# An RWKV scan with a SoLU layer behind it on one core: from word 502 of the written order on, engine orders and queues are chosen anew, five squares are halved by GpSimd, and four state sums move from TensorE to VectorE

## The chip, the cores and the metric

The kernel runs on one core of a Trainium2 chip. The core has TensorE (PE in the profile, matrix products; its weight loads are shown as PEld), VectorE (DVE), ScalarE (ACT), GpSimd (POOL), and SyncE (SP), which here only issues transfers. The metric is the device time of one execution in microseconds (us); lower is better.

## The reference

The input is four batches of eight heads, 768 steps, head size 48. A linear recurrence runs over the steps; its result, rows of 8 x 48 = 384 values, goes through a layer 384 -> 1024 -> 384 with a SoLU (a softmax times its own input), a layer norm and a gain. In float32:

```python
for t in range(S):                                   # S = 768, for 4 batches and 8 heads
    cur = einsum('bhd,bhe->bhde', u * k[t], v[t])
    y[t] = einsum('bhd,bhde->bhe', r[t], state + cur)
    state = w[t][..., None] * state + einsum('bhd,bhe->bhde', k[t], v[t])
x = y as 3072 rows of 384
h = x @ w_in
sm = softmax(h); solu = h * sm
ln = (solu - mean(solu)) / sqrt(var(solu) + 1e-6) * g_ln
out = ln @ w_out
```

## The kernel before

The 768 steps are cut into 6 chunks of 128, so there are 24 units of work (chunk, batch); unit i is chunk i // 4 of batch i % 4, and unit i needs the state that unit i - 4 left. Everything that the kernel does is one step of one unit, and the order of the steps is written out by hand: the string `ORDER` (line 21) is a list of words such as `Oa17.7`, which means step `Oa` of unit 17 with the option `7`. The loop at line 698 reads the words one after another and calls the step's function. The class `InOrder` (line 70) chains the instructions of each engine, so that each engine executes its instructions exactly in the order of the words; nothing is reordered by a scheduler. Between engines only data and buffers order the work. A buffer is one of a ring (4 to 10 deep, line 67), so a step also waits until the unit that had the buffer before is through with it. PSUM has eight banks, and the digit in an option of a TensorE step is the bank that it writes.

The steps of a unit, with the engine of each, in the order in which one unit goes through them:

- `LW LK LR LV`: the loads, 192 KB each, issued by SP, or by GpSimd (`.g`) or ScalarE (`.a`). `lw`, `ex` (ScalarE): logarithm and exponential of the decays. `cum` (TensorE): two products that sum the logarithms. `kp` (VectorE): k and r times the decays. `kt` (SP): both turned by a transposing transfer (in the first units TensorE does it instead).
- `p`, `q` (GpSimd), `dg` (VectorE), `dv` (GpSimd): the bonus term of u. `vb`: v as bf16, by ScalarE (`.a`) or GpSimd (`.p`).
- `M` (TensorE) and `m` (VectorE): the scores within the chunk and their mask. `Y` (TensorE) and `y`: the chunk's result. With the option `i` the bonus is added by a TensorE product and `y` is copied by ScalarE; else `y` is a VectorE addition.
- `S` (TensorE), `et` (ScalarE), `st` (VectorE): the new state. `S` makes the decay of the chunk and the sum over its steps, and adds the old state with a product with the identity (lines 458 to 480). With the option `n` that product is left out, and `st` (lines 482 to 489) adds the old state on VectorE and then multiplies by the decay; without `n`, `st` is the multiplication alone.
- the turning of y: `X` (three TensorE products) and `xT` (a copy), or `xt` (a transposing transfer by SP).
- `H` (TensorE), `e` (ScalarE, exponential), `he` (VectorE, h times e), `hq` (ScalarE, square): the hidden layer, with the 1024 values along partitions, so 24 products of 128 columns. A unit that has an `ht` word (`by_rows`, line 501) is computed the other way round, with six products of 512 columns, row sums taken by ScalarE, and `he` turned back by a transposing transfer.
- `Oa`, `Ob` (TensorE, lines 610 to 640): the output, in two halves of four blocks. Each block has a product of 386 columns for the output, a narrow one (2 columns) for the sum of e, and a narrow one (1 column) for the sum of the squares. For a unit with a word `ea`, GpSimd adds the two halves of e beforehand and half of the narrow products of e fall away. For a unit with a word `qa` the same holds for the squares:

```python
def square_add(i, x):
    pool.tensor_add(out=hq[:, :KF // 2, :], in0=hq[:, :KF // 2, :], in1=hq[:, KF // 2:, :])
...
if i not in paired:                       # paired: the units with a word qa
    pe.matmul(o_ps[:, DM + 2:], lhsT=hq[:, f, :], rhs=one_col[:, :1], ...)
elif f % 2 == 0:
    pe.matmul(o_ps[:, DM + 2:], lhsT=hq[:, f // 2, :], rhs=one_col[:, :1], ...)
```

- `qm`, `lv`, `rs`, `o`, `out`: variance, its root, the scaled output and the store by SP. Unit 23, the last, is cut in halves (`HA HB EA EB DA DB QA QB`), and its store is shared by ScalarE and SP.

The order before has no `qa` word and no state with `n`. All instructions are recorded by the one helper at line 86, so the profile shows L86 for nearly all of them, and the tiles tell them apart.

Of the kernel before, what the change touches and what calls it, by code (L numbers as in the profile page):

```python
# [41 lines left out]
out5 lw19 dg10 e6 p13 kt15 H7.3 dv11 LV13 LW21.g xT8.a q12 he6 e7 vb12.p H8.6 hq6.a lw16 st11 he7 kt13 dg12  # L42
M12.1 X9.0 Oa6.5 p15 xT9.a dv10 Y11.n3 lw18 LK20.g m12.d Ob6 e8 p14 y11.d qm6 LV17 hq7.a he8 lv6 Y10.n2 LK18
M15.0 m15.d q13 rs6 y10.d dv12 q14 q15 H9.3 Oa7.7 Ob7 o6.a X10.0 LV14.a e9 LV16.g out6 hq8.a xT10.a he9 Y12.n5
p17 lw21 vb15.p vb14.p hq9.a xt11 qm7 y12.d M14.1 S10.3 Oa8.0 cum16.4 m14.d LK21.g et10 lv7 S12.1 st10 rs7
LK19.g LW22 dg15 dg13 Ob8 LR19.g vb13.a xt12 cum18.2 o7.a et12 ex16 H11.6 qm8 lv8 st12 kp16 out7 ex18 rs8 dv15
o8.a e11 dv13 S15.1 et15 dg14 H12.4 ea11.p e12 kp18 vb17.a q17 LR21 vb16.a out8 LV19.g LV21 lw22 he11 kt16
LV18.g hq11.a S13.3 p16 st15 Oa9.0 LR22.g Y15.n7 he12 LR20 y15.d Ob9 LK22 q16 M13.4 cum21.1 qm9 lv9 m13.d ex21
kp21 H10.6 p19 xt15 et13 rs9 Oa11.5 o9.a cum19.0 e10 Ob11 p18 st13 he10 qm11 hq12.a ex19 dg17 out9 Y13.n2 Oa12.4
Ob12 lv11 lw20 y13.d kt18 hq10.a rs11 dv14 vb19.p q18 M16.2 kt17 X13.7 kp19 Y14.n6 qm12 p21 vb18.a LK23 S16.0  # L50
xT13.a S14.7 lv12 rs12 o12.a m16.d y14.d cum20.1 et16 out12 et14 dg16 st14 q19 H13.3 H15.6 dg18 st16 ex20 xt14
o11.a Oa10.5 kp20 e13 dv16 M17.0 out11 ea13.p he13 dg19 cum22.2 e15 p20 ex22 dv17 Y16.i4 he15 Ob10 kp22 y16.a
H14.6 hq13.a e14 qm10 LW23.g q20 p22 M18.3 dv18 q22 ea15.p S18.2 LV20 lv10 kt19 m17.d Y17.n1 m18.d hq15.a Oa13.0
y17.d et18 dg20 st18 Ob13 rs10 he14 M19.3 ea14.p o10.a xt16 vb20.p qm13 H16.1 e16 kt22 dv20 Y18.n6 X17.5 m19.d
lv13 kt20 y18.d out10 xT17.a q21 rs13 Oa15.7 LV22.g Ob15 he16 M20.4 qm15 hq14.a S17.3 lv15 m20.d H17.1 dg21 et17
st17 kt21 M21.5 dv19 rs15 LR23 o15.a e17 m21.d Oa14.4 Ob14 he17 lw23 o13.a qm14 cum23.5 Y19.n3 xt18 Y20.n7 ex23
y19.d lv14 out15 y20.d ht16 LV23 ea17.p vb22.p rs14 vb21.a o14.a H18.0 p23 e18 X20.2 dg22 M22.3 S19.7 hq17.a
kp23 xT20.d m22.d Oa16.6 sv16 dv21 Y21.n5 hq16.a sv18 vb23.a Ob16 sq16 et19 H20.2 out13 he18 q23 y21.d dg23 dv22
e20 st19 xt19 he20 H19.0 Y22.n5 Oa17.7 kt23 e19 dv23 qm16 Ob17 y22.d ht18 M23.4 xt21 he19 lv16 rs16 o16.d Oa18.3
Ob18 hq20.a H21.0 hq18.a hq19.a m23.d ht20 xt22 out14 sq18 sv20 qm18 e21 lv18 ea19.p Y23.n2 rs18 Oa19.6 qm17  # L60
ea21.p lv17 rs17 y23.d Ob19 he21 Oa20.5 hq21.a qm19 out16 H22.0 o17.d xt23 lv19 o18.d rs19 Oa21.2 HA23.3 Ob21
out18 HB23.4 e22 Ob20 o19.d EA23 he22 hq22.a EB23 qm21 sq20 DA23 ea22.p lv21 qm20 lv20 DB23 QB23.d rs21 Oa22.7
QA23.a rs20 out17 Ob22 qm22 o20.a out19 lv22 Oa23.6 o21.d rs22 Ob23.s34 out20 out21 o22.a qm23 lv23 rs23 out22
o23.a out23.h
"""

NIO, NLW, NKP, NWK, NHT = 7, 10, 6, 4, 4
# [664 lines left out]
```

## Time and profile before

| what | value |
|---|---|
| median of 3 runs | 143.83 us (143.63 to 145.34) |
| the profiled execution, its own time | 144.28 us |
| span of the program in the profile | 142.5 us |
| busy: PE, DVE, ACT, POOL | 126.0, 122.7, 118.6, 118.4 us |
| TensorE clock granted, mean | 0.992 |

The span runs from the first instruction of the program to the last; the execution's own time has 1.8 us more around it. A row of the timeline gives the start of an instruction, its length, engine, operation, and output <- inputs. Matmuls overlap: a row of 0.33 us can be followed by the next 0.16 us later. What a group of matmuls costs TensorE is therefore read from the start of the group to the start of the next one. The same holds, less strongly, for the other engines.

### The profile page before, as it was taken

The numbers are of one execution on the slowest core, as the hardware profiler recorded it, in microseconds if no ns is written. First come the engines' busy times: TensorE is split into PE (matmuls) and PEld (weight loads), VectorE is DVE, ScalarE is ACT, GpSimd is POOL, SyncE is SP. The second block draws the span as 40 slices with busy tenths as digits, with TensorE's granted clock in tenths as the row PEclk, the third lists the DMA queues.
The fourth block names the chain that finished last, engine by engine and source line by source line (L and its number), as shares of the span: only waits on it lengthen the run. The fifth ranks groups of instructions, "written<-read, shape, count | busy, mean of one in ns | idle before, by whom it ended". The sixth has DMA issues, their size and how long they took to land.

```text
span 142.5 us, 4827 instructions
## 1 busy us (share of the span) xinstructions
PE 126.0 (88%) x1901; PEld 95.7 (67%) x1906; DVE 122.7 (86%) x203; ACT 118.6 (83%) x243; POOL 118.4 (83%) x152
## 2 busy tenths in 40 slices
PE   0598966968999999999969999999999999999970
PEld 0146545657967887669858797788866766787760
DVE  6147889996999999999987999899999999878760
ACT  3658799959999999999986989998677889897780
POOL 7999999979999999999999999999999693402300
PEclk9999999999999999999999999999999999999996
DMA  4999999999999999999999899999999897562314
GB/s 93 272 300 346 316 282 384 389 293 225 249 249 244 290 250 294 246 224 230 234 191 278 197 230 212 281 158 223 176 218 208 134 246 80 136 182 68 127 59 167
DMA packets 94713, 31.98 MB, mean 224 GB/s; under 512 B 88585, under 2 KB 92818, under 8 KB 94690
## 3 DMA queue, kind: packets, MB, share of 16 engines
q1 hardware_dynamic: 70578, 20.79, 67.9%
q10 hardware_dynamic: 22128, 4.79, 15.6%
q0 software_dynamic: 1984, 6.10, 14.1%
q8 instruction: 15, 0.25, 0.7%
q14 instruction: 8, 0.07, 0.1%
HBM read 22.03 MB, written 4.72 MB: 188 GB/s over the span
## 4 chain that ended last, share of the span: by engine, by line
PE 48%; DMA 16%; POOL 14%; ACT 10%; DVE 5%; issue 3%; ACTq 0%; POOLq 0%; DVEq 0%
PE ps L86 48%; DMA win_f<-in_moe_w_in_dram 5%; DMA kr<-kp 5%; DMA kr_in<-in_r_dram 4%; POOL w L86 3%; DMA xT<-y 3%; POOL q L86 2%; ACT ps L86 2%; ACT hq L86 2%; POOL win_sb L86 1%; POOL p L86 1%; ACT e L86 1%; DVE kr L86 1%; POOL dv L86 1%; DVE he L86 1%
## 5 line engine op out<-in xcount | busy, mean ns | idle before, releaser
L86 PE MATMUL ps<-w,he 128*128 128x386 bf16 (+4 forms) x208 | 43.5, 312 | 0.0
L86 PE MATMUL ps<-xT,win_sb 128*128 128x128 bf16 x504 | 31.2, 219 | 0.2 <-DVE kr L86 0.2
L86 ACT ACTIVATE e<-ps 128x1024 bf16<-128x1024 f32 (+1 forms) x25 | 24.6, 987 | 7.5 <-PE ps L86 6.6
L86 PEld LDWEIGHTS <-win_sb 128*128 128x128 bf16 x504 | 29.0, 98 | 1.8 <-DVE kr L86 0.3
L86 DVE TENSOR_TENSOR kp<-ps,kr_in 128x768 bf16<-128x768 f32 x24 | 22.6, 950 | 7.9 <-DMA kr_in<-in_r_dram 4.2
L86 DVE TENSOR_TENSOR he<-ps,e 128x1024 bf16<-128x1024 f32 (+1 forms) x22 | 25.6, 1170 | 2.2 <-ACT e L86 1.9
L86 DVE TENSOR_TENSOR m<-ps,keep 128x1024 bf16<-128x1024 f32 x22 | 26.6, 1215 | 0.8 <-PE ps L86 0.7
L86 PE MATMUL ps<-one_col,hq 128*128 128x1 bf16 x168 | 26.7, 164 | 0.0
L86 POOL TENSOR_TENSOR p<-kr_in 128x384 bf16<-128x384 f32 x24 | 23.9, 1003 | 0.3
L86 ACT ACTIVATE hq<-he 128x1024 bf16<-128x1024 bf16 (+1 forms) x21 | 21.6, 1031 | 0.7 <-DVE he L86 0.7
L86 POOL TENSOR_TENSOR dv<-vb,dg 128x384 bf16<-128x384 bf16 x24 | 19.8, 829 | 2.6 <-DVE dg L86 2.3
L86 POOL TENSOR_TENSOR q<-p,u_bc 128x384 bf16<-128x384 bf16 x24 | 21.7, 914 | 0.1
L86 PEld LDWEIGHTS <-he 128*128 128x128 bf16 x208 | 19.1, 96 | 3.5
L86 ACT ACTIVATE ps<-ps 128x768 f32<-128x768 f32 x24 | 19.0, 796 | 2.4 <-PE ps L86 2.2
L86 PEld LDWEIGHTS <-hq 128*128 128x128 bf16 x168 | 14.1, 96 | 8.3
L86 POOL TENSOR_TENSOR ea<-e 128x512 bf16<-128x512 bf16 x9 | 10.3, 1150 | 9.4 <-ACT e L86 9.4
L86 ACT ACTIVATE lw<-w_in 128x384 bf16<-128x384 f32 x24 | 12.3, 521 | 5.5 <-DMA w_in<-in_w_dram 5.5
L86 PE MATMUL ps<-inv_col,e 128*128 128x2 bf16 x96 | 15.1, 165 | 0.0
L86 PEld LDWEIGHTS <-kp 128*128 128x128 bf16 x176 | 12.2, 104 | 3.9 <-DVE kp L86 2.1
L86 PEld LDWEIGHTS <-kr 64*128 64x128 bf16 (+1 forms) x272 | 10.3, 96 | 6.1 <-issue 1.8
L86 DVE TENSOR_REDUCE dg<-q 128x8 f32<-128x384 bf16 x24 | 12.8, 542 | 0.0
L86 POOL DMA_DIRECT2D kr_in<-in_r_dram x12 | 11.0, 921 | 0.3 <-POOL p L86 0.3
(97 smaller groups left out, 271.5 us busy)
## 6 DMA issues: line engine op xcount, KB each, us to landing
out_dram<-o SPq DMA_DIRECT2D x23, 192.0 KB, 3.2
kr_in<-in_k_dram SPq DMA_DIRECT2D x13, 192.0 KB, 5.1
kr_in<-in_r_dram POOLq DMA_DIRECT2D x12, 192.0 KB, 5.1
w_in<-in_w_dram SPq DMA_DIRECT2D x11, 192.0 KB, 5.2
kr_in<-in_r_dram SPq DMA_DIRECT2D x10, 192.0 KB, 5.3
v_in<-in_v_dram SPq DMA_DIRECT2D x10, 192.0 KB, 5.5
v_in<-in_v_dram POOLq DMA_DIRECT2D x9, 192.0 KB, 4.2
w_in<-in_w_dram ACTq DMA_DIRECT2D x8, 192.0 KB, 3.6
```

The costliest lines, as they stand in the source:

```text
L86: made = make(*args, **kwargs)
```

## The change

Only `ORDER` changes. Its first 501 words (up to `Y12.n5`) stay, and with them every engine's program up to there, which in the profile is the time up to about 78 us. Behind them all words are placed anew:

- `qa` for units 14, 16, 17, 19 and 21 (GpSimd halves their squares).
- `S12`, `S13`, `S17` and `S19` get `n`: the old state is added by VectorE.
- Unit 16 loses `ht`, `sv` and `sq`: it goes the usual way instead of by rows. It gets `ea`; so does unit 12, while 11 and 14 lose theirs.
- Units 11 and 12 are turned by TensorE (`X`, `xT`) instead of a transfer, unit 17 by a transfer instead of TensorE.
- Twelve instead of eight loads go to GpSimd's queue behind the split (`.g`). `vb14`, `vb15` and `vb20` go from GpSimd to ScalarE, `vb17` and `vb23` the other way; `y16` goes from ScalarE to VectorE, `y18` the other way; `xT20` and `o16` go from VectorE to ScalarE.
- The engines' orders, the queues' orders and the banks behind the split are new.

```diff
@@ -42,26 +42,26 @@
 out5 lw19 dg10 e6 p13 kt15 H7.3 dv11 LV13 LW21.g xT8.a q12 he6 e7 vb12.p H8.6 hq6.a lw16 st11 he7 kt13 dg12
 M12.1 X9.0 Oa6.5 p15 xT9.a dv10 Y11.n3 lw18 LK20.g m12.d Ob6 e8 p14 y11.d qm6 LV17 hq7.a he8 lv6 Y10.n2 LK18
 M15.0 m15.d q13 rs6 y10.d dv12 q14 q15 H9.3 Oa7.7 Ob7 o6.a X10.0 LV14.a e9 LV16.g out6 hq8.a xT10.a he9 Y12.n5
-p17 lw21 vb15.p vb14.p hq9.a xt11 qm7 y12.d M14.1 S10.3 Oa8.0 cum16.4 m14.d LK21.g et10 lv7 S12.1 st10 rs7
-LK19.g LW22 dg15 dg13 Ob8 LR19.g vb13.a xt12 cum18.2 o7.a et12 ex16 H11.6 qm8 lv8 st12 kp16 out7 ex18 rs8 dv15
-o8.a e11 dv13 S15.1 et15 dg14 H12.4 ea11.p e12 kp18 vb17.a q17 LR21 vb16.a out8 LV19.g LV21 lw22 he11 kt16
-LV18.g hq11.a S13.3 p16 st15 Oa9.0 LR22.g Y15.n7 he12 LR20 y15.d Ob9 LK22 q16 M13.4 cum21.1 qm9 lv9 m13.d ex21
-kp21 H10.6 p19 xt15 et13 rs9 Oa11.5 o9.a cum19.0 e10 Ob11 p18 st13 he10 qm11 hq12.a ex19 dg17 out9 Y13.n2 Oa12.4
-Ob12 lv11 lw20 y13.d kt18 hq10.a rs11 dv14 vb19.p q18 M16.2 kt17 X13.7 kp19 Y14.n6 qm12 p21 vb18.a LK23 S16.0
-xT13.a S14.7 lv12 rs12 o12.a m16.d y14.d cum20.1 et16 out12 et14 dg16 st14 q19 H13.3 H15.6 dg18 st16 ex20 xt14
-o11.a Oa10.5 kp20 e13 dv16 M17.0 out11 ea13.p he13 dg19 cum22.2 e15 p20 ex22 dv17 Y16.i4 he15 Ob10 kp22 y16.a
-H14.6 hq13.a e14 qm10 LW23.g q20 p22 M18.3 dv18 q22 ea15.p S18.2 LV20 lv10 kt19 m17.d Y17.n1 m18.d hq15.a Oa13.0
-y17.d et18 dg20 st18 Ob13 rs10 he14 M19.3 ea14.p o10.a xt16 vb20.p qm13 H16.1 e16 kt22 dv20 Y18.n6 X17.5 m19.d
-lv13 kt20 y18.d out10 xT17.a q21 rs13 Oa15.7 LV22.g Ob15 he16 M20.4 qm15 hq14.a S17.3 lv15 m20.d H17.1 dg21 et17
-st17 kt21 M21.5 dv19 rs15 LR23 o15.a e17 m21.d Oa14.4 Ob14 he17 lw23 o13.a qm14 cum23.5 Y19.n3 xt18 Y20.n7 ex23
-y19.d lv14 out15 y20.d ht16 LV23 ea17.p vb22.p rs14 vb21.a o14.a H18.0 p23 e18 X20.2 dg22 M22.3 S19.7 hq17.a
-kp23 xT20.d m22.d Oa16.6 sv16 dv21 Y21.n5 hq16.a sv18 vb23.a Ob16 sq16 et19 H20.2 out13 he18 q23 y21.d dg23 dv22
-e20 st19 xt19 he20 H19.0 Y22.n5 Oa17.7 kt23 e19 dv23 qm16 Ob17 y22.d ht18 M23.4 xt21 he19 lv16 rs16 o16.d Oa18.3
-Ob18 hq20.a H21.0 hq18.a hq19.a m23.d ht20 xt22 out14 sq18 sv20 qm18 e21 lv18 ea19.p Y23.n2 rs18 Oa19.6 qm17
-ea21.p lv17 rs17 y23.d Ob19 he21 Oa20.5 hq21.a qm19 out16 H22.0 o17.d xt23 lv19 o18.d rs19 Oa21.2 HA23.3 Ob21
-out18 HB23.4 e22 Ob20 o19.d EA23 he22 hq22.a EB23 qm21 sq20 DA23 ea22.p lv21 qm20 lv20 DB23 QB23.d rs21 Oa22.7
-QA23.a rs20 out17 Ob22 qm22 o20.a out19 lv22 Oa23.6 o21.d rs22 Ob23.s34 out20 out21 o22.a qm23 lv23 rs23 out22
-o23.a out23.h
+S12.n6 qm7 LR21.g X11.4 lv7 LW22 vb15.a LR20.g M14.1 p16 hq9.a LR19.g y12.d xT11.d LK19.g Oa8.0 rs7 m14.d vb13.a
+X12.3 et12 LK21 Ob8 cum16.4 LW23 o7.a S10.1 dg15 xT12.a dg13 ex16 cum18.2 qm8 et10 dv15 st12 kp16 st10 lv8 ex18
+H11.6 p18 rs8 kt16 o8.a H12.4 kp18 LV19.g Y15.n1 dg14 e11 Oa9.0 out8 vb14.a he11 Ob9 e12 M13.6 lw22 p17 lw21
+y15.d he12 cum21.2 kt17 S15.1 qm9 q16 LK22 S13.n4 out7 m13.d ea12.p vb16.a hq11.a dv14 dg16 ex21 Oa11.5 LV18.g
+et13 et15 kp21 H10.6 dv13 q17 st15 xt15 hq12.a st13 Y13.n3 cum19.1 lv9 lw20 Ob11 e10 p19 ex19 p20 he10 rs9
+Oa12.4 kp19 y13.d Ob12 o9.a qm12 M16.1 m16.d kt18 hq10.a LR22.g lv12 qm11 rs12 S16.0 o12.a X13.3 xT13.a S14.6
+dv16 kt21 lv11 lw23 Y14.n7 dg17 y14.d et16 et14 st16 cum20.1 rs11 st14 H13.3 Y16.n0 q18 q20 out9 q19 ex20 kp20
+y16.d vb17.p e13 H15.6 out12 o11.a M17.0 e15 ea13.p he13 dg19 Oa10.5 he15 hq13.a Ob10 cum22.3 vb18.a S18.2 qm10
+ea15.p xt14 kt19 xt16 m17.d lv10 LV21.g rs10 H14.6 Oa13.0 et18 vb19.p dg18 dv17 Y17.n1 p21 dv18 ex22 kp22 o10.a
+st18 hq15.a M18.4 Ob13 out11 y17.d kt20 m18.d p22 e14 out10 H16.1 LV20.g qm13 M19.4 lv13 rs13 o13.a xt17 dv19
+Y18.i3 he14 e16 Oa15.7 y18.a m19.d Ob15 he16 hq14.a M20.3 hq16.a LK23 M21.5 LR23.g xt18 q21 qm15 m20.d H17.0
+lv15 Y19.n2 qa14.p m21.d Oa14.4 e17 dg21 rs15 y19.d he17 vb20.a qa16.p o15.a LV22.g dg20 cum23.5 Ob14 S17.n7
+ex23 ea16.p kp23 Y20.n2 out13 H18.0 LV23.g qm14 kt22 et17 dv20 hq17.a Oa16.6 y20.d vb21.a p23 dv21 st17 X20.3
+q22 lv14 Ob16 xt19 Y21.n7 e18 rs14 qa17.p o14.a he18 M22.4 xT20.a qm16 y21.d out15 dg22 hq18.a m22.d kt23 H20.2
+e20 ht18 xt21 he20 vb22.p ea17.p H19.0 Y22.n5 vb23.p dv22 Oa17.7 e19 he19 lv16 Ob17 y22.d ea19.p M23.2 q23 m23.d
+ht20 dg23 Oa18.4 rs16 hq20.a o16.a S19.n5 hq19.a H21.0 Ob18 et19 qm17 qa19.p e21 sq18 st19 he21 lv17 Oa19.5 rs17
+dv23 sv18 sv20 Y23.n3 Ob19 xt22 out16 y23.d qm19 hq21.a qm18 ea21.p o17.d lv19 qa21.p out14 H22.1 Oa20.7 rs19
+e22 o19.d lv18 rs18 xt23 Ob20 Oa21.6 sq20 he22 hq22.a Ob21 HA23.3 HB23.1 o18.d out17 ea22.p qm20 qm21 lv21 EA23
+Oa22.5 lv20 DA23 rs21 EB23 out19 rs20 o21.d out18 DB23 QA23.a Ob22 o20.a Oa23.3 qm22 lv22 QB23.d out21 Ob23.s24
+rs22 o22.a qm23 lv23 rs23 o23.a out20 out22 out23.h
 """
 
 NIO, NLW, NKP, NWK, NHT = 7, 10, 6, 4, 4
```

## The prediction

> **What bounds the kernel now.** I read the busy tenths first, then stretches cut at the split (78 us), then the chain that ended last, then the waits behind the split.
>
> ```profile
> PE   0598966968999999999969999999999999999970
> DVE  6147889996999999999987999899999999878760
> POOL 7999999979999999999999999999999693402300
> ```
>
> ```profile
> 78.00:100.00 22.00, 22.00 (x371) 17.85 (x368) 21.43 (x35) 20.27 (x44) 21.77 (x27) 1.00 1.07 219
> 100.00:110.00 10.00, 9.88 (x157) 7.13 (x155) 10.00 (x14) 7.20 (x15) 9.90 (x12) 1.00 1.05 201
> 110.00:120.00 10.00, 9.95 (x145) 6.99 (x141) 10.00 (x16) 8.74 (x21) 7.05 (x9) 1.00 0.88 158
> 126.00:131.00 5.00, 5.00 (x81) 4.13 (x79) 3.94 (x9) 3.91 (x12) 1.15 (x1) 1.00 0.32 102
> 131.00:138.10 7.10, 7.04 (x108) 5.49 (x105) 4.83 (x10) 6.11 (x17) 1.15 (x1) 1.00 0.31 112
> 138.10:142.50 4.40, 0.00 (x0) 0.00 (x0) 0.35 (x1) 0.38 (x1) 0.00 (x0) 0.72 0.39 137
> ```
>
> ```profile
> 120.36 10.55 PE ps L86 x156
> ...
> 138.13 0.35 DVE o L86
> ```
>
> ```profile
> POOL ea L86 <- ACT e L86: 9.4, 4, 4.0
> ...
> POOL dv L86 <- DVE dg L86: 2.3, 1, 2.3
> ...
> PEld L86 <- issue: 0.5, 3, 0.2
> ...
> PEld L86 <- DMA xT<-y: 0.2, 1, 0.2
> ```
>
> The columns of the stretches are PE, PEld, DVE, ACT, POOL. Three engines are full from 78 to 110 us, VectorE to 120, GpSimd until about 112; TensorE alone is full to 138.1 us, and behind the split it waits for almost nothing (0.5 and 0.2 us). So TensorE sets the end, with 4.4 us of last outputs and stores behind it. Nothing ahead of 78 us changes. A gain can only be TensorE work taken away, its few waits, or the closing; a loss can come from any engine that falls behind TensorE.
>
> **TensorE, term by term.** I take starts, not lengths.
>
> ```profile
> 85.06 0.32 PE L86 MATMUL ps<-st,ident 128*128 128x384 bf16 x1
> ...
> 85.22 0.33 PE L86 MATMUL ps<-vb,kp 128*128 128x96 bf16 x4
> ...
> 85.39 0.33 PE L86 MATMUL ps<-w,he 128*128 128x386 bf16 x1
> ...
> 86.25 0.33 PE L86 MATMUL ps<-st,kr 128*128 128x96 bf16 x4
> ...
> 88.21 1.50 PE L86 MATMUL ps<-xT,win_sb 128*128 128x128 bf16 x24
> ...
> 89.55 0.33 PE L86 MATMUL ps<-w,he 128*128 128x386 bf16 x1
> ...
> 90.36 0.32 PE L86 MATMUL ps<-lw,uti_neg 128*128 128x384 bf16 x1
> ...
> 93.96 0.34 PE L86 MATMUL ps<-ident,y 128*128 128x128 bf16 x3
> 94.14 0.25 PE L86 MATMUL ps<-st,kr 128*128 128x96 bf16 x2
> ...
> 115.01 1.46 PE L86 MATMUL ps<-win_sb,xT 128*128 128x512 bf16 x5
> 116.30 0.28 PE L86 MATMUL ps<-ident,y 128*128 128x128 bf16 x2
> ...
> 117.36 0.82 PE L86 MATMUL ps<-w,he 128*128 128x385 bf16 x4
> 118.03 0.25 PE L86 MATMUL ps<-st,kr 128*128 128x96 bf16 x2
> ```
>
> - Four states with `n` lose the product with the identity: 85.06 to 85.22, so 4 x 0.16 = -0.64 us.
> - Five `qa` take 4 narrow products each. An output half with 12 products takes 85.39 to 86.25 = 0.86 us, one with 10 (e added beforehand) 89.55 to 90.36 = 0.81; a narrow product is 0.025 us. 20 x 0.025 = -0.50.
> - Unit 16 by columns: H 1.34 (88.21 to 89.55) for 1.29 (115.01 to 116.30), and two halves of 0.81 for two of 0.67 (117.36 to 118.03): +0.05 + 0.28 = +0.33.
> - `X11` and `X12` come, `X17` goes: one `X` is 93.96 to 94.14, +0.18.
> - `ea11` and `ea14` go, `ea12` comes (16 is counted above): 4 x 0.025 = +0.10.
>
> Sum: -0.53 us if TensorE waits as little as before.
>
> **VectorE.** An `n` costs it an addition of the old state, 128x384 out of PSUM; the nearest row is the `st` multiplication itself.
>
> ```profile
> 96.37 0.55 DVE L86 TENSOR_TENSOR st<-ps,et 128x384 bf16<-128x384 f32 x1
> 96.83 0.54 DVE L86 TENSOR_REDUCE dg<-q 128x8 f32<-128x384 bf16 x1
> ...
> 117.42 1.21 DVE L86 TENSOR_TENSOR m<-ps,keep 128x1024 bf16<-128x1024 f32 x1
> ```
>
> ```profile
> 121.69 0.29 PE L86 MATMUL ps<-st,kr 128*128 128x96 bf16 x3
> ```
>
> From start to start it is 0.46 us; the multiplication that now reads what the addition wrote cannot overlap it, so I take the whole length, 0.55: four make +2.2 us. Bounds: 4 x 0.46 = 1.84 us if they overlap, 4 x (0.55 + 0.55) = 4.4 us if the multiplication out of SBUF costs another 0.55 (the add alone is new; nothing excludes that much). Against this stand `o16` and `xT20`, which leave VectorE.
>
> What counts is how far VectorE is ahead where TensorE needs it. Take unit 22: `m22` (117.42) is done at 118.63, `Y22` (121.69) reads it, a margin of 3.06 us. Counting the words behind the split by start-to-start times (`m` and `he` 1.13, `kp` 0.87, `st`, `y`, `dg` 0.46, `qm` 0.20, the added sums 0.46), VectorE has 42.5 us of work up to and with `m22` in the new order and 39.3 in the old: three added sums, and one `he`, one `y`, one `qm` that stood behind it. TensorE reaches `Y22` 0.53 us earlier. So the margin is 3.06 - 3.2 - 0.53 = -0.7 us, -1.0 with the 0.09 us that each dependent multiplication waits. But the old VectorE time up to there holds idle time (22.00 - 21.43 = 0.57 us between 78 and 100), waits for `e` and `ex` that I don't see in the new order: `e11`, `e12`, `ex21` and `ex19` have their inputs there before `he` and `kp` ask for them. Without those the margin is -0.4 us. I take +0.3 us of new waits of TensorE, between 0 and 1.0. The places are where TensorE asks for `st17`, `m22` and the bank that `he17` frees. VectorE thereby stands level with TensorE from about 114 to 127 us; the cover is gone, and any further delay of VectorE there goes to the end one for one.
>
> **GpSimd.** Rows for its new work:
>
> ```profile
> 87.01 1.80 POOL L86 DMA_DIRECT2D v_in<-in_v_dram  x2
> 88.83 1.01 POOL L86 TENSOR_TENSOR p<-kr_in 128x384 bf16<-128x384 f32 x1
> ...
> 105.76 2.25 POOL L86 TENSOR_TENSOR ea<-e 128x512 bf16<-128x512 bf16 x2
> 107.96 0.49 POOL L86 CAST vb<-v_in 128x384 bf16<-128x384 f32 x1
> ```
>
> A `qa` has the shape and type of an `ea`: 1.10 us (105.76 to 107.96 for two), 5.5 us. Four more loads to issue, 0.91 us each (87.01 to 88.83 for two): 3.6. One cast less: -0.5. Together +8.6 us, against 9.4 + 2.3 us in which GpSimd waits behind the split. That fits, but the wait stood at the end and the work comes in the middle: in the new order 42.2 us of GpSimd work lie between 78.94 us and the end of `ea17`, so it ends at 121.1, and TensorE's `Oa17`, which needs it, starts at 120.6 us by a count of the same kind. That count puts the old `Y22` at 120.7, where the trace has 121.69, so TensorE's small waits add almost 1 us: 121.5. Level again; I take 0, bounds 0 to 2 us.
>
> **SP and the transfers.** Three transposing transfers go (`xt11`, `xt12`, `ht16`), `xt17` comes.
>
> ```profile
> DMA to landing us min/median/max: 2.3/2.7/4.3
> ```
>
> That is for `xT<-y`. `xt17` can be issued at about 105.4 us (`y17`, with `out11`, `kt20`, `out10` ahead of it in SP's queue) and lands at 108.1 to 109.7; `H17` follows at 110.1. `xt23`, the last, waits for `y23` (127.9) and lands at 130.6 to 132.2, `HA23` comes at 132.2. Loads move earlier or stay; the tightest, `LR23` on GpSimd, is issued 6 us ahead of `kp23`. Taken at 0, at most some 2 us for one transfer that lands late. In the closing SP's last three stores are now spaced by their producers, where before the queue held them:
>
> ```profile
> 92.68 0.53 SPq L86 DMA_DIRECT2D out_dram<-o  x1
> ...
> 136.71 2.90 SPq L86 DMA_DIRECT2D out_dram<-o  x4
> ```
>
> Four issues took 2.90 us where one alone takes 0.53, and the last ended at 139.61, 1.13 us behind the VectorE `o` (138.13 + 0.35); at most 1.13 - 0.53 = 0.6 us can go. Between 0 and -0.6; I take -0.2, since the queue may be as slow again.
>
> **The sum.** -0.53 (TensorE) + 0.3 (VectorE) + 0 (GpSimd) + 0 (transfers) - 0.2 (closing) = -0.4 us. Against the profiled execution (144.28 us, span 142.5) that is 143.9 and a span of 142.1; the median of the runs, 143.83, is 0.45 us below that execution, so I predict 143.4 us.
>
> **Rivals.**
> - *VectorE held by GpSimd.* The `n` multiplication has both inputs in SBUF (the sum and the decay). Hardly any VectorE operation before has that while GpSimd works, so its price shows nowhere. If the two engines exclude each other there, each of the four waits for up to one GpSimd operation, 0 to 1.1 us; `st13`, `st17`, `st19` fall where GpSimd is full. Three half operations are 1.6 us on VectorE, of which all reaches the end beyond its zero margin save about 0.3: 143.4 + 1.3 = 144.7 us. It decides as soon as VectorE is 0.3 us late.
>  The Trainium skill, page SBUF — State Buffer, section Who interferes with whom, has this as a rule: a VectorE instruction with two SBUF inputs and a GpSimd instruction that reads SBUF exclude each other for the whole instruction, and the one that issues second waits. No run here shows it yet; by that rule this rival would be the forecast.
> - *GpSimd late* (ends slower than before). `ea17` and `qa17` stand in one in-order queue behind 40 us of work without a gap; each microsecond by which it falls behind holds `Oa17`, then `qa19` and `Oa19`. It decides from 0.3 us of delay on. Price: 1.6 to 4 us, by two to four of the 1.10 us operations placed too late: 145.0 to 147.5 us. For it: the full POOL digits; against it: between 78 and 110 us GpSimd was idle for only 0.33 of 32 us, so its work can be counted on to follow without gaps.
> - *TensorE alone counts.* VectorE keeps up, the stores close 0.5 us earlier: 143.83 - 0.53 - 0.5 = 142.8 us.
> - *A transfer lands late* (`xt14`, `xt17` or `xt23`) and TensorE stands for 2 us: 145.5 us.
>
> **Chances.** Forecast (142.9 to 144.2): 0.52. VectorE held: 0.20. GpSimd late: 0.13, a third of it above 146.7. TensorE alone: 0.10. Transfer late: 0.05. The range reaches from 142.4, inside the best case, to 145.8, which leaves out most of the upper half of GpSimd late. The forecast's own range is 142.9 to 144.2. Two per cent, about what a measurement of this kernel can tell from no change, is 2.9 us: faster than 140.95 no case reaches (0.02), slower than 146.7 the ends of two (0.07), the rest 0.91.
>
> **What would show it.** The step is right if the last matmul ends at 137.5 to 138.2 us, if TensorE's new waits name `st`, `m` or `he`, and if GpSimd's idle time behind the split falls from 11.7 to about 3 us. The VectorE rival shows in `st<-sn,et` rows of over 0.7 us; GpSimd late in TensorE waits for `ea` or `hq` from POOL. A wait of TensorE of over 1 us in the stretch 78 to 110, where my count finds none, would make it wrong.

## The result and the profile after

| what | before | after |
|---|---|---|
| median of 20 runs each | 143.61 us (142.47 to 146.57) | 144.43 us (143.66 to 150.56) |
| ratio after to before | | 1.0075, 95% interval 1.0048 to 1.0102 |
| the profiled execution, its own time | 144.28 us | 144.03 us |
| its span | 142.5 us | 142.3 us |
| TensorE, first product of the new part to the last of all | 78.02 to 138.04 us | 76.53 to 139.02 us |
| from there to the end of the span | 4.43 us | 3.29 us |

The change makes the kernel slower by 0.75%, where 0.3% faster was forecast. The medians are over all runs; the ratios, here and below, leave disturbed runs out.

The profiled span is shorter all the same. In the execution of before, TensorE stood for 1.12 us just ahead of the split, for a transfer, and so began the new part late; in that of after the same transfer was in time:

```profile
74.00 0.40 PE L86 MATMUL ps<-kr 64*128 64x128 bf16 x8 [1.12 <-DMA kr<-kp]
...
78.02 0.40 PE L86 MATMUL ps<-kr 64*128 64x128 bf16 x8
```

```profile
72.60 0.40 PE L86 MATMUL ps<-kr 64*128 64x128 bf16 x8
...
76.53 0.17 PE L86 MATMUL ps<-off_blocks,halves 128*128 128x8 bf16 x1
```

(TensorE in the timeline, before and then after.) That start lies in the part that the change leaves alone, so the comparison has to be made from the split on. From there to its last product TensorE takes 60.02 us before and 62.49 after: +2.47 us. The closing behind it is 1.14 us shorter.

The stretches of the profile after, columns PE, PEld, DVE, ACT, POOL as before:

```profile
78.00:100.00 22.00, 20.82 (x355) 17.00 (x352) 21.93 (x34) 19.76 (x43) 21.90 (x25) 1.00 1.07 210
100.00:110.00 10.00, 10.00 (x175) 7.89 (x173) 10.00 (x14) 8.31 (x17) 9.85 (x13) 1.00 0.77 173
110.00:120.00 10.00, 9.55 (x137) 6.65 (x132) 9.96 (x16) 8.22 (x17) 9.94 (x11) 1.00 0.73 165
...
126.00:131.00 5.00, 4.72 (x67) 3.61 (x65) 4.77 (x10) 3.13 (x10) 3.71 (x4) 1.00 0.29 96
131.00:138.10 7.10, 6.69 (x97) 5.06 (x96) 5.11 (x11) 5.91 (x16) 1.67 (x2) 1.00 0.37 126
138.10:142.50 4.40, 0.92 (x13) 0.71 (x10) 0.47 (x2) 0.88 (x3) 0.00 (x0) 0.97 0.37 132
```

Between 78 and 100 us TensorE, full before, is idle for 22.00 - 20.82 = 1.18 us, between 110 and 120 for 0.45, between 126 and 131 for 0.28. VectorE has no hole at these places (21.93 of 22.00, 9.96 of 10.00; of the 0.23 us that it stands in the third stretch, 0.20 come at 130.65, behind the gap). Between 131 and 138.1 us TensorE stands for another 0.41. The timeline names the gaps; the number in brackets is the idle time ahead of the row, with what ended it:

```profile
82.70 1.50 PE L86 MATMUL ps<-xT,win_sb 128*128 128x128 bf16 x24 [0.69 <-DVE kp L86]
...
93.75 0.40 PE L86 MATMUL ps<-kr 64*128 64x128 bf16 x8 [0.49 <-DVE kp L86]
...
118.17 0.34 PE L86 MATMUL ps<-st,kr 128*128 128x96 bf16 x4 [0.45 <-DVE st L86]
...
128.12 0.33 PE L86 MATMUL ps<-st,kr 128*128 128x96 bf16 x4 [0.28 <-DVE st L86]
...
137.65 0.25 PE L86 MATMUL ps<-one_col,hq 128*128 128x1 bf16 x4 [0.41 <-DVE hq L86]
```

The first four are `H12` (its bank 4 is the one that `kp16` reads, and `kp16` stands right behind `st12` on VectorE), `M16` (its bank 1 is the one that `kp19` reads, with `he10` between `st13` and it), `Y21` (behind `st17`) and `Y23` (behind `st19`): each of the four gaps follows one of the four states with `n`. The fifth is a wait for the last square of unit 23, which VectorE makes (`QB23`); it comes again without `n` (0.44 us in e1, 0.42 in e7 below), so it belongs to the new order. The chain that ended last now passes through `st13`, `st17` and `st19`. In the chain of before no VectorE row stands between 78 and 130.91 us; from there on ScalarE and VectorE take turns to the end. The last two states in the chain of after:

```profile
117.05 1.08 DVE st L86
118.17 5.85 PE ps L86 x86
...
126.86 1.22 DVE st L86
128.12 6.15 PE ps L86 x80
```

And VectorE's groups by form give the price of the new work:

```profile
L86 DVE TENSOR_TENSOR st<-ps,et 128x384 bf16<-128x384 f32 x16 | 8.6, 547 | 0.4 <-ACT et L86 0.4
L86 DVE TENSOR_TENSOR st<-sn,et 128x384 bf16<-128x384 f32 x4 | 4.5, 1120 | 0.1
L86 DVE TENSOR_TENSOR sn<-ps,st 128x384 f32<-128x384 f32 x4 | 2.2, 546 | 0.0
```

The addition costs what it was taken at, 546 ns. The multiplication behind it does the same arithmetic as the other sixteen, but takes 1120 ns in place of 547. Against GpSimd, two of the four look so (VectorE's rows of the timeline of after, then GpSimd's; the row of `win_f` is `he18`, a unit by rows, which is kept in that tile):

```profile
90.77 0.92 DVE L86 TENSOR_TENSOR st<-sn,et 128x384 bf16<-128x384 f32 x1
...
117.05 1.07 DVE L86 TENSOR_TENSOR st<-sn,et 128x384 bf16<-128x384 f32 x1
118.04 1.21 DVE L86 TENSOR_TENSOR win_f<-ps,e 128x1024 bf16<-128x1024 f32 x1
```

```profile
90.43 0.84 POOL L86 TENSOR_TENSOR dv<-vb,dg 128x384 bf16<-128x384 bf16 x1
91.22 1.25 POOL L86 TENSOR_TENSOR q<-p,u_bc 128x384 bf16<-128x384 bf16 x1
...
116.88 0.82 POOL L86 TENSOR_TENSOR dv<-vb,dg 128x384 bf16<-128x384 bf16 x1
117.66 1.23 POOL L86 TENSOR_TENSOR q<-p,u_bc 128x384 bf16<-128x384 bf16 x1
```

The multiplication issued at 90.77 ends at 91.69, 0.42 us after the `dv` that was running when it began (91.27); the one of 117.05 ends at 118.12, 0.42 us after its `dv` (117.70). The `q` behind each takes 1.25 and 1.23 us, where the 24 of them take 0.94 on the mean. So it looks as if VectorE waits for GpSimd's operation to end, and GpSimd's next one for VectorE in turn; the experiments test it.

### The profile page after: what moved, and what is told of

The parts are those of the page before. It is cut to its first block, busy times and chain, and to the rows that moved or that the text cites. A ratio compares the mean times of both kernels' runs of the same rounds, so it can differ in the third digit from the quotient of the medians.

```text
span 142.3 us, 4862 instructions
## 1 busy us (share of the span) xinstructions
PE 127.2 (89%) x1919; PEld 97.1 (68%) x1919; DVE 126.2 (89%) x206; ACT 119.5 (84%) x242; POOL 127.9 (90%) x160
## 4 chain that ended last, share of the span: by engine, by line
PE 45%; DVE 24%; ACT 9%; issue 6%; POOL 6%; DMA 6%; ACTq 1%; DVEq 0%; POOLq 0%
PE ps L86 45%; DVE kp L86 5%; DVE st L86 4%; DMA w_in<-in_w_dram 4%; DVE he L86 3%; DVE dg L86 3%; DVE m L86 3%; ACT e L86 3%; DVE y L86 2%; ACT ps L86 2%; DMA kr_in<-in_k_dram 2%; ACT w L86 2%; POOL kr_in L86 1%; ACT lw L86 1%; DVE sn L86 1%
## 5 line engine op out<-in xcount | busy, mean ns | idle before, releaser
L86 PE MATMUL ps<-xT,win_sb 128*128 128x128 bf16 x528 | 32.7, 219 | 0.9 <-DVE kp L86 0.7
L86 PEld LDWEIGHTS <-win_sb 128*128 128x128 bf16 x528 | 30.3, 98 | 2.5 <-issue 1.0
L86 DVE TENSOR_TENSOR he<-ps,e 128x1024 bf16<-128x1024 f32 (+1 forms) x23 | 26.8, 1170 | 2.3 <-ACT e L86 2.1
L86 PE MATMUL ps<-one_col,hq 128*128 128x1 bf16 x156 | 24.7, 164 | 0.4 <-DVE hq L86 0.4
L86 ACT ACTIVATE hq<-he 128x1024 bf16<-128x1024 bf16 (+1 forms) x22 | 22.8, 1035 | 2.4 <-DVE he L86 2.3
L86 POOL TENSOR_TENSOR q<-p,u_bc 128x384 bf16<-128x384 bf16 x24 | 22.3, 940 | 0.1
L86 PEld LDWEIGHTS <-he 128*128 128x128 bf16 x208 | 18.5, 96 | 3.1
L86 PE MATMUL ps<-inv_col,e 128*128 128x2 bf16 x104 | 16.4, 165 | 0.0
L86 POOL DMA_DIRECT2D kr_in<-in_r_dram x15 | 13.8, 919 | 0.3 <-POOL p L86 0.3
L86 ACT ACTIVATE o<-ps,rs 128x384 f32<-128x384 f32 (+1 forms) x19 | 10.9, 571 | 0.6 <-ACT rs L86 0.2
```

Source lines behind the costliest of these rows:

```text
L86: made = make(*args, **kwargs)
```

## The experiments

Two accounts stood against each other at first. The first is that the multiplication with two inputs in SBUF is held by GpSimd's operations, and VectorE, which has no margin, passes the delay to TensorE. The other is that GpSimd, filled by the `qa`, delays the rest. With them goes the question whether the additions alone would cost as much wherever their result is put. All ratios are to the kernel before, run on the same chip.

| run | what it changes | median | ratio, 95% interval |
|---|---|---|---|
| e1_no_n | changed kernel, no `n` | 143.43 | 0.9972 (0.9929 to 1.0015) |
| e2_sum_in_psum | changed, the sum stays in PSUM | 144.74 | 1.0004 (0.9957 to 1.0052) |
| e3_no_qa | changed, no `qa` | 144.55 | 1.0034 (0.9999 to 1.0070) |
| e4_before_with_n | before, with the four `n` | 145.98 | 1.0111 (1.0054 to 1.0168) |
| e5_before_n_psum | before, with `n`, sum in PSUM | 144.91 | 1.0058 (1.0026 to 1.0089) |
| e6_before_stores_swapped | before, `out21` ahead of `out20` | 144.96 | 1.0017 (0.9974 to 1.0060) |
| e7_no_n_no_qa | changed, neither | 142.91 | 0.9949 (0.9912 to 0.9987) |
| e8_decay_in_psum | changed, the decay stays in PSUM | 143.80 | 1.0001 (0.9969 to 1.0034) |
| e9_no_n_again | as e1 | 143.35 | 0.9960 (0.9932 to 0.9988) |
| e10_no_n_no_qa_again | as e7 | 143.25 | 0.9933 (0.9901 to 0.9964) |
| e11_before_o21_early | before, `o21` earlier | 145.84 | 1.0116 (1.0071 to 1.0161) |
| e12_changed_again | the changed kernel | 145.21 | 1.0085 (1.0048 to 1.0122) |
| e13_before_o21_early | before, `o21` and `out17` earlier | 144.19 | 1.0024 (0.9986 to 1.0061) |
| e14_stores_close | e7, stores side by side | 143.46 | 0.9949 (0.9909 to 0.9988) |

### Without the four added sums

```diff
-S12.n6 ... S13.n4 ... S17.n7 ... S19.n5
+S12.6  ... S13.4  ... S17.7  ... S19.5
```

> The changed kernel without n in its four states: the product with the identity is back on TensorE (+0.64 us), the four additions leave VectorE. Theory 1 (the multiplication st<-sn,et, with both inputs in SBUF, is held by GpSimd: its rows are 1.12 us long where st<-ps,et is 0.55, so n costs VectorE 4 x 1.1 us, and VectorE sets TensorE's pace): about 1 us less than the changed kernel, a ratio to before of 0.997 to 1.002, TensorE's waits for st and he gone. Rival (GpSimd falls behind under the five halved squares): ratio stays at 1.005 to 1.012, waits for ea and hq.

```profile
L86 DVE TENSOR_TENSOR st<-ps,et 128x384 bf16<-128x384 f32 x20 | 10.7, 550 | 0.8 <-ACT et L86 0.8
```

0.9972, and in a second trial on another chip (e9) 0.9960, beside 1.0085 for the changed kernel itself there (e12). All twenty multiplications take 550 ns on the mean, and none of the four gaps of TensorE is left. The four `n` cost 1.0 to 1.3% of the time, more than the whole loss. They do so although they save TensorE 0.64 us by the prediction's count.

> The changed kernel without n once more. Theory 1: 0.6 to 1.2% under the changed kernel on the same chip (ratio to before 0.995 to 1.001).

> The changed kernel once more, beside the next two on the same chip. Ratio to before 1.005 to 1.010 as first measured; theory 1 and its rivals say the same here, it is the yardstick.

### The sum left in PSUM

```diff
-dve.tensor_add(out=sn_t[i % 2], in0=total, in1=st_t[b][(c - 1) % 2])
-total = sn_t[i % 2]
+dve.tensor_add(out=total, in0=total, in1=st_t[b][(c - 1) % 2])
```

> The changed kernel with the sum written back to PSUM instead of SBUF: the same number of VectorE operations, but the multiplication has one input in SBUF. Theory 1: st falls from 1.12 to about 0.55 us though GpSimd works as before, ratio to before 0.994 to 1.001. If an operation of float32 out of SBUF, or two dependent ones, were slow by themselves, st would be 0.55 here too, but its end in the changed kernel would not lie 0.4 us behind the end of a GpSimd operation each time. Rival (GpSimd late): ratio as the changed kernel's, 1.005 to 1.010.

```profile
L86 DVE TENSOR_TENSOR st<-ps,et 128x384 bf16<-128x384 f32 x20 | 10.9, 552 | 0.5 <-ACT et L86 0.3
```

1.0004. The additions are all there (4 at 556 ns), the order is the changed one, only the place of the sum differs, and the multiplication is back at 552 ns. By the middle values that alone recovers nearly all of the 0.75%, though the interval reaches up to 1.0052. Against e1, on the same chip, 0.3% remains for the additions themselves, inside the intervals; in the trace TensorE still waits twice for a state, 0.49 and 0.40 us. What about SBUF was slow it doesn't yet say.

### The decay left in PSUM

The exponential is written in place, and the multiplication reads the sum from SBUF, still as float32, and the decay from PSUM:

```diff
+out_et = decay if live[i]["apart"] else et_t[i % NWK]...
-act.activation(out=et_t[i % NWK]..., in_=live[i]["s_ps"][:, DM:], func=EXP)
+act.activation(out=out_et, in_=decay, func=EXP)
...
+if live[i]["apart"]:
+    et = live[i]["s_ps"][:, DM:]
```

> The changed kernel, where in its four states with n the decay stays in PSUM, so that the multiplication reads the sum out of SBUF (float32) and the decay out of PSUM. Theory 1 (two SBUF inputs): the four multiplications 0.55 to 0.6 us, ratio 0.996 to 1.004. Rival (a float32 operand out of SBUF, just written, is slow by itself): 0.9 to 1.3 us as in the changed kernel, ratio 1.005 to 1.010.

VectorE's group, one row of its timeline, and what GpSimd does meanwhile:

```profile
L86 DVE TENSOR_TENSOR st<-sn,ps 128x384 bf16<-128x384 f32 x4 | 2.2, 554 | 0.1
```

```profile
117.22 0.55 DVE L86 TENSOR_TENSOR st<-sn,ps 128x384 bf16<-128x384 f32 x1
```

```profile
117.03 0.83 POOL L86 TENSOR_TENSOR dv<-vb,dg 128x384 bf16<-128x384 bf16 x1
117.82 0.90 POOL L86 TENSOR_TENSOR q<-p,u_bc 128x384 bf16<-128x384 bf16 x1
```

1.0001, clear of the changed kernel's interval, and 554 ns, in the middle of a `dv` of GpSimd, and the `q` behind it takes 0.90 us again. The sum still comes out of SBUF and is still float32. So it is neither the type nor SBUF as such, but two inputs in SBUF while GpSimd works.

### The added sums in the order before

```diff
-S12.1  ... S13.3  ... S17.3  ... S19.7
+S12.n1 ... S13.n3 ... S17.n3 ... S19.n7
```

> The kernel before with nothing changed but n in the same four states (12, 13, 17, 19). Theory 1: four additions and four held multiplications, 4.4 us on VectorE, eat its margin of 3 us at unit 22 and more: ratio to before 1.002 to 1.008 although TensorE has 0.64 us less to do. Rival (n is harmless, the damage is GpSimd's or the new order's): 0.994 to 0.998.

```profile
L86 DVE TENSOR_TENSOR st<-sn,et 128x384 bf16<-128x384 f32 x4 | 3.3, 820 | 0.1
```

```profile
113.63 0.56 DVE L86 TENSOR_TENSOR st<-sn,et 128x384 bf16<-128x384 f32 x1
122.85 0.89 DVE L86 TENSOR_TENSOR st<-sn,et 128x384 bf16<-128x384 f32 x1
```

```profile
112.47 0.84 POOL L86 TENSOR_TENSOR dv<-vb,dg 128x384 bf16<-128x384 bf16 x1
114.11 1.15 POOL L86 TENSOR_TENSOR ea<-e 128x512 bf16<-128x512 bf16 x1 [0.79 <-ACT e L86]
...
122.50 0.83 POOL L86 TENSOR_TENSOR dv<-vb,dg 128x384 bf16<-128x384 bf16 x1 [2.41 <-DVE dg L86]
```

1.0111, more than expected. The single rows fit all the same: the multiplication that starts while GpSimd is idle takes 558 ns, the one that starts inside a `dv` ends 0.41 us after it. A third, 558 ns, fell beside GpSimd's issuing of a load. The fourth (90.96 us, 1277 ns) doesn't fit: it began while GpSimd issued a load, and went on into the `q` that followed at 91.70; it ended 0.56 us, a whole length, behind the end of that issue (91.68). Why that one was held is open. TensorE's longest waits there name `y` (0.63 and 0.71 us) and `m` (0.45 us), the operations that stand behind the states on a VectorE that was full from 100 to 120 us already; one more is for a transfer of y (0.42 us).

### The order before, sums added in PSUM

The edits of the two runs above together.

> The kernel before with n in the same four states, and the sum written back to PSUM. In the run with the sum in SBUF two of the four multiplications were long (1.28 and 0.89 us, the others 0.56). Theory 1 (two SBUF inputs are held by GpSimd, and the addition itself also costs VectorE): all four 0.55 us, about 1 us less on VectorE, ratio to before 1.003 to 1.009, under the 1.0111 of the sum in SBUF. If the hold were all of the price: 0.994 to 0.998. If only the additions counted: 1.011 as with the sum in SBUF.

```profile
L86 DVE TENSOR_TENSOR st<-ps,et 128x384 bf16<-128x384 f32 x20 | 10.9, 549 | 0.8 <-ACT et L86 0.7
L86 DVE TENSOR_TENSOR ps<-ps,st 128x384 f32<-128x384 f32 x4 | 2.2, 554 | 0.0
```

```profile
82.02 1.50 PE L86 MATMUL ps<-xT,win_sb 128*128 128x128 bf16 x24 [1.48 <-DMA xT<-y]
```

1.0058: about half of what the same `n` cost there with the sum in SBUF (the intervals, 1.0026 to 1.0089 and 1.0054 to 1.0168, overlap a little). That agrees with two costs, the hold and the additions themselves on an engine that is full. But that the additions alone outweigh the 0.64 us that TensorE saves is not shown: in the profiled execution TensorE waits 0.45 us for `m`, and 1.48 us for the transfer of unit 11's y (the last row), whose word stands ahead of `S12`, the first word that the edit touches. How often that transfer is late in the runs without a profile is not on record.

### Without the five halved squares

```diff
-qa14.p ... qa16.p ... qa17.p ... qa19.p ... qa21.p
```

> The changed kernel without its five qa: GpSimd has 5.5 us less, TensorE 0.5 us more. Rival (GpSimd late): faster than the changed kernel by 0.5 to 1 us. Theory 1 (VectorE sets the pace): the waits for VectorE hide the 0.5 us of TensorE, and st<-sn,et stays near 1.1 us, at most a little less where GpSimd now has gaps: ratio to before 1.005 to 1.010.

```profile
L86 DVE TENSOR_TENSOR st<-sn,et x4: 627/996/1369, 80.8 to 127.2; 128x384 bf16<-128x384 f32 x4
```

1.0034 (0.9999 to 1.0070). The middle lies under the range of theory 1 (1.005 to 1.010) and, against the changed kernel's 1.0075, 0.4% (0.6 us) lower, as the rival had it; the interval reaches into both, so this run doesn't decide. The multiplications are long without any `qa`, so the `qa` are not what holds them. The minimum, 627 ns, is the multiplication of unit 19: it began when only 0.21 us of GpSimd's `dv` was left, and ended 0.42 us behind it as the others did. That one is 0.58 us shorter than in the changed kernel (1.21). So what an `n` costs hangs on where it happens to meet GpSimd.

### Neither sums nor squares

> The changed kernel without n and without qa: the new orders and queues alone. The kernel without n alone stood at 0.9972. Theory 1 with TensorE as the bound: 20 narrow products of 0.025 us come back, +0.5 us, ratio 0.999 to 1.003. If the halved squares cost by GpSimd as much as they save: 0.995 to 0.998.

> The changed kernel without n and without qa once more, the fastest so far (0.9949). If the halved squares cost more waits than the 0.5 us of TensorE that they save: 0.1 to 0.4% under the kernel without n alone. If the first difference was chance: equal to it or 0.1 to 0.4% above.

The stretches of e7:

```profile
78.00:100.00 22.00, 22.00 (x372) 17.84 (x371) 21.20 (x33) 20.72 (x45) 21.90 (x25) 1.00 1.12 218
...
110.00:120.00 10.00, 10.00 (x148) 7.18 (x145) 9.38 (x15) 8.60 (x18) 8.45 (x11) 1.00 0.96 184
```

0.9949, and again 0.9933: the rest of the change (the new order, unit 16 by columns, the moves between engines and queues), with neither of the edits that were to save TensorE work, is the fastest of all and beats both kernels. I had expected 0.999 to 1.003, by counting the 0.5 us of narrow products that come back. That was a miss; the other account, 0.995 to 0.998, came nearer. TensorE is at 22.00 of 22.00 and 10.00 of 10.00. Against the runs with `qa` and without `n` that is 0.9949 to 0.9972 on two chips, and 0.9933 to 0.9960 side by side on one: twice about 0.25% the same way, though the intervals overlap. The `qa` save nothing that these runs could show, and perhaps cost a little.

Where this gain sits: from the end of `Y12` to its last product TensorE takes 60.8 us in e7 and in e10, in place of 59.95 in before and 60.35 in e13, the order before but for two stores. The closing behind the last product takes 3.3 us in both, in place of 4.43 and 4.77. So in the profiled executions the new order isn't shorter on TensorE; it gains in the closing.

### The stores at the end

What made the closing 1.1 us shorter was tried from three sides. In e6 `out21` goes ahead of `out20`. In e11 and e13 `o21` is made earlier in the order before, so that the last stores are spaced; e13 has `out17` ahead of it as well, because both use the same buffer of the ring, and in e11 `out17` stores what `o21` has written, unit 21's rows in place of unit 17's, and waits for it. In e14 the stores of units 20 and 21 are put next to each other in e7, with `o21` later and `QB23` earlier.

```diff
-QB23.d rs21 ... rs20 out17 Ob22 ... Oa23.6 o21.d rs22 Ob23.s34 out20 out21
+rs21 out17 o21.d QB23.d ... rs20 Ob22 ... Oa23.6 rs22 Ob23.s34 out21 out20
```

(That is e13.)

> The kernel before with the words out20 and out21 swapped, nothing else. From the last matmul to the end of the span it took 4.43 us before and 3.29 us in the changed kernel, since the issue of out21, right behind out20, took 1.5 us and the last two stores queued behind it. If the order of these two stores decides: 3.3 to 3.7 us, ratio to before 0.992 to 0.997. If the length comes from elsewhere: 4.4 us, ratio 0.998 to 1.002.

> The kernel before, where o21 and its store come about 0.8 us earlier (VectorE does o21 ahead of the last square QB23, ScalarE rs21 ahead of it, SP out21 ahead of out20), as in the changed kernel. The closing behind the last matmul was 4.1 to 4.6 us in four orders of the kernel before and 3.3 us in all of the changed kernel, and in the long ones the second of two stores issued 0.4 us apart took 1.2 to 1.7 us. If that nearness makes the closing long: 3.3 to 3.7 us, ratio to before 0.992 to 0.998. If not: 4.2 us or more, ratio 0.999 to 1.003.

> The kernel before with o21 ahead of the last square QB23 and out21 ahead of out20, and the store of unit 17 ahead of o21, so that the output is whole. If two stores issued 0.4 us apart make the closing long: now they are some 0.5 to 0.8 us apart, closing 3.3 to 3.7 us, ratio to before 0.992 to 0.998. If not: 4.1 us or more, ratio 0.999 to 1.004.

> The changed order without n and qa (0.993 to 0.995), but with o21 behind qm22 and the stores out20 and out21 right behind one another ahead of o22, as in the kernel before. If nearness makes the closing long: 4.1 to 4.6 us, ratio to before 0.999 to 1.004. If not: 3.3 to 3.5 us, ratio 0.993 to 0.997.

e6 1.0017, e13 1.0024, e14 0.9949 as e7: none differs. In e13 the stores were spaced and the closing was 4.77 us all the same; in e14 they were adjacent and it was 3.69, above the 3.3 of e7 but under every closing of the order before. So how close the stores stand doesn't explain it. (The closing of e4, 5.0 us, lies outside the 4.1 to 4.6 that the expectation of e11 names for the order before.) e11 says nothing on it: its `out17` became one more late store (closing 5.93 us, 1.0116).

What does go with a slow store is something else. The queue named "instruction", none of the kernel's own, brings 16 KB every 8 to 10 us. Its row in narrow windows of the transfers (before from 137 to 138 us, after from 135 to 136, e13 from 136 to 137), with the issues of that window and their median time to landing where there are any:

```profile
q8 instruction: 1, 0.02, 6.7%
...
out_dram<-o SPq DMA_DIRECT2D x2, 192.0 KB, 2.9
```

```profile
q8 instruction: 1, 0.02, 8.2%
```

```profile
q8 instruction: 1, 0.02, 5.7%
...
out_dram<-o SPq DMA_DIRECT2D x1, 192.0 KB, 3.9
```

In before and e13 the last stores are under way with it and take 2.9 and 3.9 us to land. In the changed kernel it starts at 135.89 and ends at 137.20, one store (136.22) takes 2.35 us, and the last three, issued from 138.10 on, land after 1.7 to 1.8. Over the ends of all sixteen traces, where they give the landing, a store that is issued ahead of this transfer or early in it lands after 2.2 to 4.2 us, the others after 1.5 to 2.3, but for one of 2.65 right behind it. This is a coincidence of times and was not tried by itself: no edit moves this transfer alone.

## Why the prediction was wrong

The sum was -0.53 (TensorE) + 0.3 (VectorE) + 0 (GpSimd) + 0 (transfers) - 0.2 (closing). The profiles give, from the split on, +2.47 on TensorE and -1.14 at the end; as the two executions met the split in different conditions, the 20 runs of each are the better total: +0.82 us between the medians, +1.1 by the ratio of 1.0075.

- **TensorE's work, -0.53: held.** Counted again by start-to-start steps in the trace of after, the products behind the split take 0.52 us less than before.
- **VectorE, +0.3: this step failed.** It said "the nearest row is the `st` multiplication itself" and took 0.55 us for each `n`, +2.2 us in all. That row reads one input from PSUM and one from SBUF; the new multiplication reads two from SBUF. From the start of each addition to the start of what follows the multiplication, the four take 1.79, 1.42, 1.57 and 1.71 us (79.91 to 81.70, 90.20 to 91.62, 116.47 to 118.04, 126.28 to 127.99), in place of 0.46: +4.65 us, above even the upper bound of 4.4. The margin, already counted as used up, turned this into waits of TensorE: 2.47 + 0.53 = 3.0 us in the profiled pair, of which the four gaps shown make 1.91 and the wait for `QB23` 0.41. Part of the 3.0 is the pair's own, since VectorE and GpSimd ran ahead while TensorE stood in before. e13, the order before but for two stores, started the new part as early as after and took 60.35 us from the end of `Y12`, where before took 59.95 and after 62.33; against it the waits are 2.5. All five gaps are waits for VectorE.
- **The rival "VectorE held by GpSimd" was what happened,** with its place, its sign (`st<-sn,et` rows over 0.7 us) and by the number with its price: 144.7 us forecast, 144.43 measured. That the number fits so well is luck. The rival took 1.6 us of new waits of TensorE in all (0.3 + 1.3) and a closing of -0.2; the waits were 2.5 and the closing -1.15, and the two errors cancel. It left `st12` out, which was held the longest (1.28 us). The Trainium skill, page SBUF — State Buffer, section Who interferes with whom, states the rule: two SBUF inputs on VectorE against a GpSimd instruction that reads SBUF, and the later one waits for the whole of the other. The traces agree: the four end 0.41 to 0.43 us after GpSimd's operation, and with one input moved to PSUM (e8, e2) they take 0.55; the one row that doesn't follow is the 1277 ns of e4. The rival was given 0.20, because no row of before showed it; no row spoke against it either. A new kind of operands has no nearest row, and the prediction wrote down the bound but took the value at the low end.
- **"GpSimd late": not seen.** Behind the split no wait of TensorE names GpSimd, and GpSimd's own waits fell from 11.7 to 2.5 us (1.3 + 0.8 for the squares, 0.4 for `e`), near the 3 forecast:

```profile
POOL hq L86 <- ACT hq L86: 1.3, 1, 1.3
PE ps L86 <- DVE kp L86: 1.2, 2, 0.7
POOL hq L86 <- ACT et L86: 0.8, 1, 0.8
PE ps L86 <- DVE st L86: 0.7, 2, 0.4
...
POOL ea L86 <- ACT e L86: 0.4, 1, 0.4
```

- **Where it would be wrong:** a wait of over 1 us in the stretch 78 to 110 was named as the sign. It is there, 1.18 us, for `kp16` and `kp19`. `st`, `m` and `he` were named as what TensorE would ask for; `kp`, which stands behind two of the four states in VectorE's order, was left out, and so was the last square `QB23`. The prediction also read that TensorE sets the end up to 138.1 us; the chain of before leaves TensorE at 130.91 us and runs through ScalarE and VectorE from there.
- **The transfers, 0: held.** No wait of TensorE names one behind the split.
- **The closing, -0.2: right sign, wrong size.** In the trace of after:

```profile
138.10 1.73 SPq L86 DMA_DIRECT2D out_dram<-o  x2
...
139.12 0.35 DVE L86 TENSOR_SCALAR o<-ps,rs 128x128 f32<-128x128 f32 x1 [0.90 <-PE ps L86]
```

 The last issue ends at 139.83, 0.36 us behind the last `o` (139.47), where before it was 1.13: -0.77, all and more of the "at most 0.6". From there to the end of the span it is 2.48 in place of 2.86 us: -0.38, a term that the prediction did not have. The two make -1.15.

So two terms were mis-sized: VectorE cost some 2.2 us more than taken, the closing brought 0.9 more, and together with the forecast's -0.4 they make about +0.9 us. So it is luck, too, that 144.43 us lies only 1.0 us above the forecast: without the closing's 0.9 it would have been twice as far, and the cause of that gain stays open. The sign of the change was lost on VectorE.

## What to carry to other kernels

When work moves to VectorE beside a busy GpSimd, look at where each input lies before taking a price from a row of the same shape: with two inputs in SBUF an operation took 0.92 to 1.28 us in the changed kernel, with one of them in PSUM 0.55, and keeping the sum or the decay in PSUM was a change of a few lines. Count margins before saving work on the bounding engine: 0.64 us off TensorE cost 1.0 to 1.3% of the time, hold included, because VectorE had none to give. When a new order comes together with new edits, try it without them: here the rest of the change was a gain (0.9949 and 0.9933), and the edits put on top of it took it away.

## What the runs showed of the hardware beyond that

- The hold goes both ways: the GpSimd arithmetic behind a held multiplication is longer by about 0.3 us (`q` 1.23 to 1.25 against 0.94 on the mean of all 24, and 0.90 at the same place in e8).
- A store under way while the "instruction" queue brings 16 KB lands after 2.2 to 4.2 us in place of 1.5 to 2.3, at the ends of sixteen traces; that the one causes the other is argued and not shown.
